# Four weight tiles loaded and turned by quarters, inverse tables turned in one visit, and a re-phased backward second step

## The chip, the cores and the metric

The kernel runs on one core of a Trainium2 chip. The metric is device time in microseconds (us) of one execution; lower is better. Engines are named as the profile names them: PE is TensorE (PEld its weight loads), DVE is VectorE, ACT is ScalarE, POOL is GpSimd, SP is SyncE, which here only issues DMAs.

## What is computed

A transformer block (a spectral mixer followed by a token-mixing MLP, both with pre-LayerNorm and residual) and all its gradients, from bf16 inputs:

```python
def _A_ref(x, w_r, w_i):                       # spectral mixer, S = 2048, D = 448
    X = rfft2(x.astype(float32), axes=(-2, -1))
    y = irfft2(X * (w_r + 1j * w_i), s=(S, D)).astype(bfloat16)
def _B_ref(x, w1, b1, w2, b2):                 # MLP over tokens, F = 1792
    u = einsum("bsd,sf->bdf", layernorm(x), w1) + b1
    y = einsum("bdf,fs->bds", gelu(u), w2) + b2
    return y.transpose(0, 2, 1)
h  = x + _A_ref(layernorm(x), w_r, w_i)
h2 = h + _B_ref(h, w1, b1, w2, b2)             # with a LayerNorm of h inside
out, vjp = jax.vjp(f, x, w_r, w_i, w1, b1, w2, b2)
return out, *vjp(grad_out)                     # 8 outputs
```

## The kernel before

The order on TensorE, VectorE, ScalarE and SP is written by hand: each engine runs its instructions in the program's order. Where the code calls `evac`, a running estimate of the load of the two engines chooses whether ScalarE or VectorE empties a PSUM bank, so a moved step can move an evacuation from one engine to the other. PSUM is eight banks, four called `ps_mm` (long accumulations) and four called `ps_ff` (everything short).

The stages, with the times at which TensorE is in them:

- Opening (0 to 49 us). The rows of x are normalised and put through the first step of the FFT, 16 row tiles t. `row_a(t)` is four 128x128 products of a folded pair of rows (`fold_prep` or `fold_quarters`, VectorE) with `Rs[t]` (`scale_R`, VectorE: the table `Rm` times the row's 1/std). `row_b(h)`, three tiles behind, is four products with the table `csF`. `csF` is made once: a sine on ScalarE, then two flips of it on VectorE, then a 2-element copy on ScalarE over the first column (`gen_fwd_d`, run at t = 1 from `cs_ops`). The tables `Ut` and `Vt` come in pieces from `gen_UV` (VectorE, with a sine each on ScalarE).
- Between these, `fill(n)` takes n steps of the generator `dg_gen`: dgu = w2 . grad_out, 14 tiles j of w2 by 16 products t, each 128x448, 224 steps in all. `FILL_A[t]` and `FILL_B[t]` say how many steps stand in row tile t behind `row_a(t + 1)` and at its end. A product needs tile j of w2 transposed. Tiles 0 to 4 are loaded as they lie (`load_w2T`, 512 KB each) and turned on TensorE (`turn_w2`: 16 transposes of 128x128 into PSUM, ScalarE copies them to SBUF); tiles 5 to 13 come through a DMA that transposes. The first 32 steps alternate between tiles 0 and 1 by quarters of four t, since grad_out also arrives by quarters. The ring `w2T_ring` has five places, so the load of tile 5 is issued when tile 0 has been used up, and so on.
- `gen_inv_s(a)` turns the tables Ut and Vt for the inverse: 32 products of 32x32 for each a, at t = 10, 11, 12 and 13. `gen_RT` turns a permuted copy of `Rm` at t = 2.
- Forward second step (`s2_stage`, 49 to 73 us): for each of four sets s, 48 products in 32x32 groups (`four`), four evacuations, `fill(n1)`, the second `four` of the set before, a multiplication by the spectral weights on VectorE, `fill(n2)`; a fifth round closes the last set.
- Inverse rows and LayerNorm of h, the MLP forward, its backward (76 to 225 us).
- Backward: rows of the FFT, `s2_stage` again (240 to 281 us) with `bwd_mult` on VectorE, then `inv_rows` with the gradient of x. `fill` takes its steps from two generators `gw_gen` here (gradients of w2 and w1, 196 and 224 steps). One period of `gw_gen` is 14 steps: six products of 128x128 weights, then one step with four products of 64-row groups (`parts`, two at a time side by side), one empty step, six more products. `N_FILL_B[2]` steps are filled ahead of the backward second step, `N_FILL_B[4]` behind it, `N_FILL_B[5]` in each inverse row; what is left is run by `drain` at the end. 28 steps are filled in the rows before `N_FILL_B[2]`.

SP's queue in the opening, in order: x tiles 0 and 1 (224 KB), w2 tile 0 (512 KB), x 2 and 3 (224 KB), grad_out quarter 0 (448 KB), w2 tile 1, x 4 to 7 (448 KB), grad_out quarters 1, 2 and 3, w2 tile 2, x 8 to 11, w2 tile 3, x 12 to 15, a 2 KB tail of grad_out, two bias loads, w2 tile 4, then the spectral weights W, mixed with the transposing loads and the reshapes of the rows (`resh`). Eight DMAs are in flight at most: each waits for the one eight places ahead to land.

20 dummy products of zeros run on TensorE at the start (L375).

## Time and profile before

Three runs took 340.55, 341.36 and 341.02 us, median 341.02. The profiled execution took 340.96 us; its span, from the first to the last instruction, is 339.2 us, so 1.76 us lie outside it. The profile comes from that execution.

| stretch (us) | stage | TensorE busy (us) | VectorE busy | ScalarE busy | DMA GB/s |
|---|---|---|---|---|---|
| 0 to 6.3 | dummies, first loads | 5.08 | 4.91 | 3.56 | 213 |
| 6.3 to 15.6 | rows, up to row_a(4) | 7.75 of 9.30 | 8.88 | 8.05 | 388 |
| 15.6 to 32.8 | rows, up to row_a(10) | 16.04 of 17.20 | 16.53 | 12.29 | 209 |
| 32.8 to 49.2 | last rows, tables | 16.36 of 16.40 | 10.43 | 11.46 | 230 |
| 49.2 to 76 | forward second step, rest of dg | 26.45 of 26.80 | 16.77 | 17.75 | 164 |
| 76 to 95 | inverse rows | 18.40 of 19.00 | 15.25 | 17.11 | 258 |
| 95 to 238.5 | MLP, backward rows | 143.5 of 143.5 | 98.62 | 64.39 | |
| 238.5 to 281 | backward second step | 42.32 of 42.50 | 36.88 | 31.38 | 241 |
| 281 to 326 | backward inverse rows | 45.00 of 45.00 | 36.16 | 34.68 | 263 |
| 326 to 339.2 | rest of gw, last stores | 9.41 of 13.20 | 8.18 | 5.52 | 246 |

Read it so: a product counts as busy until its result is out, so a busy TensorE can still lose time between two starts. The weight loads (PEld) show when a product could start.

### The profile page before, as it was taken

What the parts mean: (1) busy time and instruction counts of PE and PEld (TensorE: products, weight loads), DVE (VectorE), ACT (ScalarE), POOL (GpSimd) and SP (SyncE); (2) the same over time, 40 slices, a digit from 0 to 9 for tenths busy, and PEclk for the clock granted to TensorE, in tenths of its full rate; (3) what the DMA queues carried; (4) which work ended last, traced back from release to release, by engine and by line L of the source; (5) the groups of instructions that cost most, each with busy time, mean ns of one, the idle gap of its engine ahead of it and who ended that gap; (6) DMA issues with size and microseconds to landing.
All of it is one profiled execution on the core that took longest, in us unless ns stands there. A gap on an engine that the chain in (4) does not pass through costs nothing.

```text
span 339.2 us, 7995 instructions
## 1 busy us (share of the span) xinstructions
PE 330.3 (97%) x2893; PEld 174.0 (51%) x2893; DVE 252.6 (74%) x678; ACT 206.2 (61%) x447; POOL 83.9 (25%) x255
## 2 busy tenths in 40 slices
PE   8898999999999999999999999999999999999995
PEld 4565665456545555555555555555334344555552
DVE  8999649726947888594226988787598984599994
ACT  6886766858965544523132346665488875688882
POOL 7755602331310000000001111210002222156660
PEclk9999999999999999999999999999999999999999
DMA  7979999949999999787986989636998999969785
GB/s 250 399 195 183 228 245 196 167 110 261 252 366 305 337 277 241 179 259 197 187 192 154 188 176 165 171 83 203 262 254 280 184 227 281 349 164 295 233 309 198
DMA packets 136142, 78.03 MB, mean 230 GB/s; under 512 B 86568, under 2 KB 127512, under 8 KB 135976
## 3 DMA queue, kind: packets, MB, share of 16 engines
q1 hardware_dynamic: 133576, 73.59, 82.6%
q0 software_dynamic: 2528, 3.95, 5.5%
q8 instruction: 22, 0.36, 0.5%
q14 instruction: 16, 0.13, 0.2%
HBM read 28.33 MB, written 22.04 MB: 149 GB/s over the span
## 4 chain that ended last, share of the span: by engine, by line
PE 85%; DVE 6%; ACT 3%; DMA 2%; SPq 2%; issue 1%; POOL 0%; DVEq 0%; ACTq 0%
PE ps_mm L220 73%; PE ps_ff L220 8%; PE ps_ff L225 4%; DMA rA<-in_A_x_dram 2%; ACT rO L84 2%; DVE r L84 2%; DVE stats L84 1%; SPq L329 1%; SPq L310 1%; DVE rS L84 1%; DVE rA L84 1%; ACT rAT L84 0%; DVE rD L84 0%; DVE rX L84 0%; DVE rB L84 0%
## 5 line engine op out<-in xcount | busy, mean ns | idle before, releaser
L220 PEld LDWEIGHTS <-r 128*128 128x128 bf16 (+2 forms) x628 | 58.4, 104 | 47.6 <-issue 3.0
L220 PEld LDWEIGHTS <-rS 128*128 128x128 bf16 (+1 forms) x468 | 36.3, 97 | 33.4 <-issue 7.7
L84 ACT CAST rO<-ps_mm 128x512 bf16<-128x512 f32 (+1 forms) x69 | 36.9, 584 | 14.6 <-PE ps_mm L220 13.0
L220 PE MATMUL ps_mm<-rD,r 128*128 128x448 bf16 x224 | 44.5, 352 | 0.0
L220 PEld LDWEIGHTS <-rst 128*128 128x128 bf16 (+1 forms) x320 | 23.6, 97 | 31.3 <-issue 14.0
L731 POOL DMA_DIRECT2D r<-r x30 | 17.8, 601 | 66.5 <-ACT r L84 59.3
L220 PE MATMUL ps_mm<-rC,rE 128*128 128x448 bf16 x144 | 32.1, 353 | 0.5 <-DMA rC<-in_grad_out_dram 0.4
L220 PE MATMUL ps_mm<-rB,r 128*128 128x448 bf16 x160 | 31.2, 352 | 0.1
L220 PE MATMUL ps_mm<-rG,rst 128*128 128x512 bf16 (+1 forms) x128 | 28.7, 380 | 0.2 <-ACT rO L84 0.2
L220 PE MATMUL ps_mm<-r,rst 128*128 128x512 bf16 (+2 forms) x144 | 27.4, 345 | 0.0
L84 ACT ACTIVATE r<-ps_mm,rstd_h 128x448 bf16<-128x448 f32 x16 | 10.1, 633 | 26.8 <-PE ps_mm L220 26.8
L84 ACT CAST r<-ps_ff 128x452 bf16<-128x452 f32 x43 | 23.2, 589 | 4.5 <-PE ps_ff L225 2.1
L84 DVE SCALAR_TENSOR_TENSOR r<-ps_mm,b2col,r 128x448 bf16<-128x448 f32 x16 | 10.9, 682 | 19.9 <-PE ps_mm L220 19.8
L84 ACT ACTIVATE r<-rC 128x448 bf16<-128x448 bf16 x16 | 9.1, 571 | 26.7 <-DMA out_dram<-r 14.1
L1189 POOL TENSOR_SCALAR lcol<-lcol 128x1 f32<-128x1 f32 x16 | 8.5, 528 | 64.7 <-ACT r L84 64.7
L84 ACT ACTIVATE rG<-rG 128x896 bf16<-128x896 bf16 x14 | 13.3, 950 | 14.9 <-DVE rG L84 14.7
L220 PEld LDWEIGHTS <-rO 128*128 128x128 bf16 (+1 forms) x165 | 15.3, 98 | 12.2 <-ACT rO L84 0.2
L84 ACT CAST rS<-ps_ff 128x512 bf16<-128x512 f32 x31 | 18.1, 587 | 2.5 <-PE ps_ff L220 2.4
L220 PE MATMUL ps_ff<-csI,rAT 113*128 113x224 bf16 (+1 forms) x108 | 19.0, 298 | 0.4 <-ACT rAT L84 0.2
L84 DVE TENSOR_SCALAR rG<-rG 128x896 bf16<-128x896 bf16 x28 | 10.9, 388 | 10.0 <-ACT rG L84 10.0
L220 PE MATMUL ps_mm<-rC,rO 128*128 128x448 bf16 x80 | 18.1, 353 | 0.0
L84 ACT CAST rG<-ps_mm 128x512 bf16<-128x512 f32 (+1 forms) x28 | 13.8, 534 | 6.8 <-PE ps_mm L220 6.7
(202 smaller groups left out, 638.2 us busy)
## 6 DMA issues: line engine op xcount, KB each, us to landing
out_dram<-rO SPq DMA_DIRECT2D x34, 256.0 KB, 3.0
r<-in_B_w_dram SPq DMA_DIRECT2D x5, 1024.0 KB, 8.4
r<-r POOLq DMA_DIRECT2D x30, 113.0 KB, 5.4
out_dram<-rG SPq DMA_DIRECT2D x11, 256.0 KB, 3.7
r<-r SPq DMA_DIRECT2D x12, 226.0 KB, 2.5
r<-in_B_w_dram SPq DMA_DIRECT2D x3, 896.0 KB, 5.1
rS<-in_B_w_dram SPq DMA_DIRECT2D x3, 896.0 KB
rB<-in_B_w_dram SPq DMA_DIRECT2D x5, 512.0 KB, 9.8
```

Source lines behind the costliest of these rows:

```text
L84: fn(**kw)
L220: nc.tensor.matmul(out, lhsT=lhsT, rhs=rhs, start=start, stop=stop)
L225: nc.tensor.matmul(out, lhsT=lhsT, rhs=rhs, start=start, stop=stop)
L310: nc.sync.dma_start(out=w2n[j], in_=B_w2[j * P:(j + 1) * P, :].rearrange("f (t c) -> f t c", c=P))
L329: nc.sync.dma_start(out=go_tp[:, 4 * q:4 * q + 4, :], in_=go_tp_d[:, 4 * q:4 * q + 4, :])
L731: defer(RESH_LAG, lambda g=g, ab=ab, eng=eng: eng.dma_start(out=D3[rowbase(g):rowbase(g) + 29:4, :, :, :], in_=ab), ab)
L1189: gp_.tensor_scalar(out=m1, in0=ms, scalar1=-1.0 / D, scalar2=None, op0=ALU.mult)
```

## The change

Two constants, the loads and turns of the first w2 tiles, the places of some steps, and the fill counts change:

- w2 tiles 0 to 3 are loaded in eight quarters. `load_quarter(k)`, k = 2 q + p, brings columns of quarter q (four t) of the pair p (tiles 2p and 2p + 1): 256 KB in pieces of 1 KB. `turn_quarter(k)` turns these eight blocks and copies them to SBUF in one copy (the first in two). Tile 4 is loaded whole, into rD, and turned by halves (`turn_half`). All turns use `ps_ff`.
- `dg_gen` takes tiles 0 to 3 together by quarters: step n = 16 q + 4 j + i. Turns 1, 2 and 3, 4 and 5, 6 and 7 stand right behind steps 7, 15, 31 and 47, the halves of tile 4 behind 57 and 61. The loads of tiles 5 to 8 are issued behind steps 51, 55, 59 and 63.
- SP's queue becomes: x 0 and 1, quarter 0, grad_out 0, x 2 and 3, quarter 1, x 4 to 7, grad_out 1, quarters 2 and 3, x 8 to 11, grad_out 2, quarters 4 and 5, x 12 to 15, grad_out 3, quarters 6 and 7, tile 4, W. The tail of grad_out and the biases are loaded after the last rows.
- 10 dummy products at the start, two more ahead of `row_a(0)`; four dg steps now stand before `row_a(0)`, and FILL_A and FILL_B differ in the first nine tiles.
- `gen_inv_s` does all four a in one visit, behind the rows; `gen_RT` and its copies stand at t = 13.
- In the backward second step n1 is 14, n2 is 14, 28, 14, 28 and 20 by round (13 and 20 before), and 35 steps (26 before) are filled ahead of it.

```diff
--- before.py
+++ after.py
@@ -36,10 +36,10 @@
 ML_F = 4
 SIDE = 2
 CAP = 9
-N_NAT = 5
+N_QTR = 4
 U_Q = 2
 N_FILL_F = (6, 3, 20, 3, 24, 2)
-N_FILL_B = (16, 16, 26, 8, 24, 8)
+N_FILL_B = (16, 16, 35, 8, 24, 8)
 INV_SD = 1.0 / float(S * D)
 
 
@@ -298,7 +298,7 @@
 
     x_pt = A_x[0].rearrange("(p t) d -> p t d", t=NT)
     go_pt_d = grad_out[0].rearrange("(p t) d -> p t d", t=NT)
-    w2T_ring = Ring(ring(rE, 0, 3, NT, P).views + ring(rO, S, 2, NT, P).views)
+    w2T_ring = Ring(ring(rE, 0, 2, NT, P).views + ring(rO, S, 2, NT, P).views + [cut(rE, 2 * S, NT, P)])
 
     def load_w2T():
         j = w2T_ring.i
@@ -306,21 +306,44 @@
             return
         wT = w2T_ring.next()
         w2Ts[j] = wT
-        if j < N_NAT:
-            nc.sync.dma_start(out=w2n[j], in_=B_w2[j * P:(j + 1) * P, :].rearrange("f (t c) -> f t c", c=P))
+        if j < N_QTR:
+            return
+        if j == N_QTR:
+            nc.sync.dma_start(out=w2n4, in_=B_w2[j * P:(j + 1) * P, :].rearrange("f (t c) -> f t c", c=P))
             return
         nc.sync.dma_start_transpose(out=wT, in_=B_w2[j * P:(j + 1) * P, :].rearrange("f (t c) -> f t c", c=P))
 
-    def turn_w2(j, parts=((0, 8), (8, 8))):
-        for h, n in parts:
-            pt = (ps_mm if j < 2 else ps_ff)()[:].bitcast(BF16).rearrange("p (t c) -> p t c", c=P)
-            for t in range(n):
-                nc.tensor.transpose(pt[:, t, :], w2n[j][:, h + t, :], ident[:])
-            sc.copy(out=w2Ts[j][:, h:h + n, :], in_=pt[:, 0:n, :])
+    def turned():
+        return ps_ff()[:].bitcast(BF16).rearrange("p (t c) -> p t c", c=P)
+
+    def turn_half(h):
+        pt = turned()
+        for t in range(8):
+            nc.tensor.transpose(pt[:, t, :], w2n4[:, h + t, :], ident[:])
+        sc.copy(out=w2Ts[N_QTR][:, h:h + 8, :], in_=pt)
+
+    def turn_quarter(k):
+        q, p = divmod(k, 2)
+        pt = turned()
+        for t in range(8):
+            nc.tensor.transpose(pt[:, t, :], w2q[:, 2 * p + t // 4, 4 * q + t % 4, :], ident[:])
+        dst = w2pair[p][:, :, 4 * q:4 * q + 4, :]
+        if k:
+            sc.copy(out=dst, in_=pt.rearrange("p (j t) c -> p j t c", j=2))
+            return
+        for j in range(2):
+            sc.copy(out=dst[:, j], in_=pt[:, 4 * j:4 * j + 4, :])
+
+    def load_quarter(k):
+        q, p = divmod(k, 2)
+        src = B_w2[2 * p * P:(2 * p + 2) * P, :].rearrange("(j f) (t c) -> f j t c", f=P, c=P)
+        nc.sync.dma_start(out=w2q[:, 2 * p:2 * p + 2, 4 * q:4 * q + 4, :], in_=src[:, :, 4 * q:4 * q + 4, :])
 
     go_tp_d = grad_out[0].rearrange("(t p) d -> p t d", p=P)
     w2Ts = {}
-    w2n = [cut(rB, j % 4 * S, NT, P) for j in range(N_NAT)]
+    w2q = cut(rB, 0, 4, NT, P)
+    w2pair = [cut(rE, 0, 2, NT, P), cut(rO, S, 2, NT, P)]
+    w2n4 = cut(rD, 10 * 512, NT, P)
 
     def load_x(q):
         nc.sync.dma_start(out=xn[:, 4 * q:4 * q + 4, :], in_=x_pt[:, 4 * q:4 * q + 4, :])
@@ -329,21 +352,26 @@
         nc.sync.dma_start(out=go_tp[:, 4 * q:4 * q + 4, :], in_=go_tp_d[:, 4 * q:4 * q + 4, :])
 
     nc.sync.dma_start(out=xn[:, 0:2, :], in_=x_pt[:, 0:2, :])
-    load_w2T()
+    load_quarter(0)
+    load_go(0)
     nc.sync.dma_start(out=xn[:, 2:4, :], in_=x_pt[:, 2:4, :])
-    load_go(0)
-    load_w2T()
+    load_quarter(1)
     load_x(1)
     load_go(1)
+    load_quarter(2)
+    load_quarter(3)
+    load_x(2)
     load_go(2)
+    load_quarter(4)
+    load_quarter(5)
+    load_x(3)
     load_go(3)
-    load_w2T()
-    load_x(2)
-    load_w2T()
-    load_x(3)
+    load_quarter(6)
+    load_quarter(7)
+    for _ in range(N_QTR):
+        load_w2T()
     gtail = rst[0:16, 2 * P:3 * P]
     gp_.memset(gtail, 0.0)
-    nc.sync.dma_start(out=gtail[:, 0:64], in_=grad_out[0][S - 16:S, 3 * P:D])
 
 
     s1, s128, s2048 = 2.0 * _sin_scale(2), _sin_scale(128), _sin_scale(2048)
@@ -371,7 +399,7 @@
     sc.activation(out=warm, in_=warm, func=ACT.Sin)
     nc.vector.memset(rAT[:, 0:512], 0.0)
     idle = ps_mm()
-    for _ in range(20):
+    for _ in range(10):
         nc.tensor.matmul(idle[:, 0:D], lhsT=rAT[:, 0:P], rhs=rAT[:, 0:D], start=True, stop=True)
 
     pcol = col()
@@ -525,18 +553,19 @@
         mm(pt[:, 0:P], lhsT=Rp, rhs=ident[:], start=True, stop=True)
         evac(out=RTm[:], in_=pt[:, 0:P])
 
-    def gen_inv_s(a):
-        pt = ps_ff()
-        for w, src in enumerate((Ut, Vt)):
-            for x in range(4):
-                o = 32 * (4 * w + x)
-                for r in range(4):
-                    small(pt[blk(r + a & 3), o:o + 32], lhsT=src[blk(r), 8 * (x // 2) + 2 * a + x % 2, :], rhs=permI[blk(r), :],
-                          start=True, stop=True)
-        evac(out=UVT[:].rearrange("p w g m -> p (w g m)").rearrange("p (x a y) -> p a x y", x=4, a=4)[:, a],
-             in_=pt[:, 0:256].rearrange("p (x y) -> p x y", x=4))
-        if a == 3:
-            gen_neg(UTn[:], UTt)
+    def gen_inv_s():
+        uvt = UVT[:].rearrange("p w g m -> p (w g m)").rearrange("p (x a y) -> p a x y", x=4, a=4)
+        pts = [ps_ff() for _ in range(4)]
+        for a, pt in enumerate(pts):
+            for w, src in enumerate((Ut, Vt)):
+                for x in range(4):
+                    o = 32 * (4 * w + x)
+                    for r in range(4):
+                        small(pt[blk(r + a & 3), o:o + 32], lhsT=src[blk(r), 8 * (x // 2) + 2 * a + x % 2, :],
+                              rhs=permI[blk(r), :], start=True, stop=True)
+        for a, pt in enumerate(pts):
+            (ve.tensor_copy if a % 2 else sc.copy)(out=uvt[:, a], in_=pt[:, 0:256].rearrange("p (x y) -> p x y", x=4))
+        gen_neg(UTn[:], UTt)
 
     inv_cols = {}
 
@@ -735,7 +764,7 @@
                     on_mult(s, j, x[:, 2 * j:2 * j + 2], y[:, 2 * j:2 * j + 2])
             if after is not None and s in after:
                 after[s]()
-            fill(n2)
+            fill(n2[s])
         fill(gap)
 
     def gen_neg(dst, src):
@@ -812,6 +841,7 @@
 
     def load_biases():
         gp_.memset(smr, 0.0)
+        nc.sync.dma_start(out=gtail[:, 0:64], in_=grad_out[0][S - 16:S, 3 * P:D])
         nc.sync.dma_start(out=smr[0:NFB, 0, :], in_=B_b1.rearrange("(j p) -> j p", p=P))
         nc.sync.dma_start(out=smr[:, 1, :], in_=B_b2.rearrange("(j p) -> j p", p=P))
 
@@ -827,14 +857,16 @@
 
     def dg_gen():
         pgs = {}
-        turns = {(0, 3): 1, (1, 11): 2, (2, 4): 3, (3, 4): 4}
-        order = [(j, 4 * q + i) for q in range(4) for j in range(2) for i in range(4)]
-        for j, t in order + [(j, t) for j in range(2, NFB) for t in range(NT)]:
+        turns = {7: (1,), 15: (2, 3), 31: (4, 5), 47: (6, 7)}
+        order = [(j, 4 * q + i) for q in range(4) for j in range(N_QTR) for i in range(4)]
+        for n, (j, t) in enumerate(order + [(j, t) for j in range(N_QTR, NFB) for t in range(NT)]):
             if not t:
                 pgs[j] = ps_mm()
             mm(pgs[j][:, 0:D], lhsT=w2Ts[j][:, t, :], rhs=go_tp[:, t, :], start=(t == 0), stop=(t == NT - 1))
-            if (j, t) in turns:
-                turn_w2(turns[j, t], ((0, 4), (4, 4), (8, 8)) if j == 0 and t == 3 else ((0, 8), (8, 8)))
+            for k in turns.get(n, ()):
+                turn_quarter(k)
+            if n in (57, 61):
+                turn_half(2 * (n - 57))
             if t == NT - 1:
                 evac(out=dgu[:, j, :], in_=pgs.pop(j)[:, 0:D])
                 if w2T_ring.i >= cap[0]:
@@ -874,12 +906,14 @@
     fold_prep(xn, 0)
     ve.reciprocal(out=rstd_x[:, 0:2], in_=rstd_x[:, 0:2])
     Rs = {t: scale_R(t) for t in range(2)}
-    turn_w2(0, ((0, 4), (4, 4)))
+    turn_quarter(0)
+    for _ in range(2):
+        nc.tensor.matmul(idle[:, 0:D], lhsT=rAT[:, 0:P], rhs=rAT[:, 0:D], start=True, stop=True)
+    fill(4)
     row_a(0, Rs.pop(0))
     for t in range(2, 4):
         ln_stats(xn, t, mvx)
     sc.activation(out=rstd_x[:, 2:4], in_=mvx[:, 2:4, 1], func=ACT.Sqrt, bias=eps_x, scale=1.0)
-    turn_w2(0, ((8, 8),))
     fold_prep(xn, 1)
     cs_ops = []
     gen_fwd_d(cs_ops)
@@ -889,24 +923,17 @@
     uv = gen_UV()
     gen_inv_cols(0)
     gen_inv_cols(1)
-    fill(4)
     for t in (4, 5):
         ln_stats(xn, t, mvx)
     for fn in rstd_of(4, 6):
         fn()
     fill(0)
-    turn_biases, place_biases = load_biases()
     Meter.side, Meter.every, Meter.count = [], 1, 0
     GROUPS = {0: (6, 8), 1: (8, 10), 3: (10, 12), 5: (12, 14), 7: (14, 16)}
     STATS = {0: (6, 7), 1: (8, 9), **{t: (t + 8,) for t in range(2, 8)}}
-    INV_S = {10: 0, 11: 1, 12: 2, 13: 3}
     W_AT = {0: 2, 1: 1, 2: 2, 3: 1, 4: 2, **{t: 1 for t in range(5, 11)}, 11: 4}
-    for c in range(2):
-        for e in range(2):
-            sc.copy(out=Rp.rearrange("p (e a q b c) -> p c e a q b", e=2, c=2, q=8, a=2)[:, c, e],
-                    in_=Rm[:, 64 * c + 32 * e:64 * c + 32 * e + 32].rearrange("p (q a b) -> p a q b", q=8, a=2))
-    FILL_A = (4, 4, 8, 12, 6, 3, 3, 3, 3, 3, 3, 3, 3, 3, 3, 3)
-    FILL_B = (0, 0, 2, 2, 2, 2, 4, 4, 3, 2, 2, 2, 2, 2, 2, 2)
+    FILL_A = (4, 7, 9, 7, 1, 6, 2, 5, 4, 3, 3, 3, 3, 3, 3, 3)
+    FILL_B = (0, 0, 0, 0, 5, 3, 6, 4, 3, 2, 2, 2, 2, 2, 2, 2)
     for t in range(NT):
         if t == 0:
             load_w2T()
@@ -944,9 +971,11 @@
             newton_gp(mvx[:, a:b, 1], rstd_x[:, a:b], slice(a, b))
         for _ in range(W_AT.get(t, 0)):
             next(w_loads, None)
-        if t in INV_S:
-            gen_inv_s(INV_S[t])
-        if t == 2:
+        if t == 13:
+            for c in range(2):
+                for e in range(2):
+                    sc.copy(out=Rp.rearrange("p (e a q b c) -> p c e a q b", e=2, c=2, q=8, a=2)[:, c, e],
+                            in_=Rm[:, 64 * c + 32 * e:64 * c + 32 * e + 32].rearrange("p (q a b) -> p a q b", q=8, a=2))
             gen_RT()
         fill(FILL_B[t])
     for _ in uv:
@@ -960,12 +989,15 @@
     cap[0] = NFB
     while held_w2:
         held_w2.pop(0)()
-    fill(14)
+    turn_biases, place_biases = load_biases()
+    fill(8)
+    gen_inv_s()
+    fill(6)
 
     def fwd_mult(s, j, x, y):
         w_mult(x, set_of(W, s)[:, 2 * j:2 * j + 2], y, False)
 
-    s2_stage(lambda s: set_of(Xs, s), fwd_mult, 8, 8, 0, split=True)
+    s2_stage(lambda s: set_of(Xs, s), fwd_mult, 8, (8,) * 5, 0, split=True)
     sc.activation(out=warm, in_=eps_h, func=ACT.Sqrt)
     drain()
 
@@ -1350,7 +1382,7 @@
         rows(t)
     fill(N_FILL_B[2])
     Meter.slack = 7.0
-    s2_stage(lambda s: X_ring.next(), bwd_mult, 13, 20, N_FILL_B[4], {0: lambda: load_du(1), 1: lambda: (load_du(0), load_xall(0)), 2: lambda: load_xall(1), 3: lambda: load_du(2)},
+    s2_stage(lambda s: X_ring.next(), bwd_mult, 14, (14, 28, 14, 28, 20), N_FILL_B[4], {0: lambda: load_du(1), 1: lambda: (load_du(0), load_xall(0)), 2: lambda: load_xall(1), 3: lambda: load_du(2)},
              2.0 * INV_SD)
     Meter.slack = 2.0
     g_out = w_io(out_2, out_3, True)
```

## The prediction, made before the changed kernel ran

> **What bounds the kernel now.** I read the page's busy shares and chain first, then the order in time of each engine in the opening (0 to 50 us) and in the backward second step (235 to 285 us).
>
> ```profile
> PE 330.3 (97%) x2893; PEld 174.0 (51%) x2893; DVE 252.6 (74%) x678; ACT 206.2 (61%) x447; POOL 83.9 (25%) x255
> ...
> PE 85%; DVE 6%; ACT 3%; DMA 2%; SPq 2%; issue 1%; POOL 0%; DVEq 0%; ACTq 0%
> ```
>
> TensorE sets the end. The chain runs on it for 85%, and one piece of the chain (94.86 to 188.89 us) has no pause at all. So whatever TensorE loses or gains before 95 us moves the end by as much. Its pauses lie in the opening; in this view the last bracket is the idle time before a row and what ended it:
>
> ```profile
> 15.57 0.65 PE L220 MATMUL ps_ff<-rX,rS 128*128 128x128 bf16 x4 [0.78 <-DVE rS L84]
> ...
> 32.84 0.40 PE L220 MATMUL ps_ff<-rX,rS 128*128 128x128 bf16 x4
> ```
>
> These are row_a(4) and row_a(10); a third such wait, 1.01 us, stands at 30.81 (row_a(9)). After 32.84 nothing waits until the forward second step starts at 49.20. What feeds these rows is VectorE, and what ScalarE does meanwhile decides the case:
>
> ```profile
> 6.19 1.15 DVE L84 BATCH_NORM_STATS2 stats<-rA 128x6 f32<-128x448 bf16 x2 [0.20 <-DMA rA<-in_A_x_dram]
> ...
> 15.74 0.46 DVE L84 TENSOR_SCALAR csF<-csF,cols 128x224 bf16<-128x224 bf16 x2
> 16.44 1.15 DVE L84 BATCH_NORM_STATS2 stats<-rA 128x6 f32<-128x448 bf16 x2 [0.24 <-DMA rA<-in_A_x_dram]
> ```
>
> ```profile
> 16.29 0.20 ACT L84 COPY csF<-rAT 128x2 bf16<-128x2 bf16 x1 [1.08 <-DVE csF L84]
> 16.39 0.58 ACT L84 CAST rS<-ps_ff 128x512 bf16<-128x512 f32 x1
> 16.86 0.27 ACT L84 CAST RTm<-ps_ff 128x128 bf16<-128x128 f32 x1
> ...
> 17.50 1.95 ACT L84 COPY rE<-ps_ff 128x1024 bf16<-128x1024 bf16 x2
> ```
>
> From 6.19 on VectorE works without a pause down to the csF flip at 15.74, and ScalarE stands 1.08 us in its own queue, at 16.29, until that flip is done. Before the change that hurts nobody: tiles 0 and 1 of w2 were turned whole and copied by 11.7 us, so TensorE has 32 steps of dg that need no copy.
>
> **The opening, part by part.** I count dg steps from 0 and call the copy of quarter k "copy k".
>
> *Loads.* x tiles 2 and 3 move from third to fourth in SP's queue, with 928 KB ahead instead of 736. At the 277 to 362 GB/s of that stretch the 192 KB more are 0.5 to 0.7 us; I take 0.6. Bounds: 0 (the queue hides it) and 2.0, by which the first grad_out load, which ends TensorE's wait at 8.19, came later than the x load. VectorE has no slack behind this load, so all up to the flip moves with it: flip done at 16.2 + 0.6, R(2), scaled at 10.28 in the same order, ready at 10.5 + 0.6 = 11.1. The third x load comes earlier, which removes the 0.24 us before 16.44, behind the flip and so too late to help it. Fewer dummies (20 to 12) are worth nothing: row_a(0) waits for VectorE's scaled table at 6.0 anyway.
>
> *The new wait.* By program order TensorE now does 8 steps and turns 0 and 1, row_a(2) at 11.1 (0.22), seven steps (7 x 0.187 = 1.31), row_a(3) (0.22), step 15 (0.19), turns 2 and 3 (16 transposes, 0.90: the groups of 16 at 20.54 and 26.18 took 0.89). It stands at step 16 at 13.95. Step 16 needs copy 2. In ScalarE's queue that is: csF sine, the csF copy that waits for the flip, the cast of row_a(3), copy 2. So 16.39 + 0.6 = 16.99, cast 0.47 (start to start, 16.39 to 16.86), copy 0.97 (half of 1.95): 18.43. TensorE stands 4.5 us, and behind step 16 in its queue stands all the rest: rows 4 and on, and so VectorE's casts of them.
>
> *From there to row_a(10).* Steps 16 to 69 (54 x 0.187 = 10.1), 48 transposes (2.67), six row_a (1.32), six row_b at 0.40 (2.4): 16.5 us, to 34.95. Two waits come on top. Turns 4 and 5 follow step 31 and step 32 needs copy 4: TensorE is there at 18.45 + 16 steps 3.0 + 2 row_a 0.44 + 2 row_b 0.80 + turns 0.89 = 23.58, ScalarE ends copy 4 at 24.5 (cast of row_b(0) at 21.9 to 22.45, Ut's sine 0.62, cast of row_a(5) 0.47, copy 0.97): 0.95. Copy 6 the same way: 0.2. So row_a(10) at 36.1 instead of 32.84: **+3.3**. VectorE, without two rD casts (1.06) and with one ps_ff cast more (0.54), would have had its fold there at 32.8 - 0.24 - 1.06 + 0.54 + 0.6 = 32.6; it is not the bound any more.
>
> *Inverse tables in one go.* Each of the four visits (35.69, 37.47, 39.26, 41.03) starts 0.097 us late on the way into 32x32 groups and costs 0.09 on the way out, by the starts of its neighbours. Three visits fall away: **-0.56**. The last evacuations are covered by the six steps (1.1 us) before the second step; uncovered they cost two copies of 0.37. RT and its four copies move to t = 13, where nothing waits for ScalarE: 0.
>
> *Queue SP.* The tail of grad_out and two bias loads leave SP's opening and stand before the last three transposed loads; their users come 20 us later: 0. The transposed loads of tiles 5 to 8 start at step 51 instead of 28; step 51 comes at 30, the first use (step 80) at 39.6, issue takes 2.1 to 2.5 and landing 5.2: covered by some 2 us; uncovered, the shortfall is paid in full (bound +1). The x load that ends VectorE's wait at 16.44 closed 4.7 MB of the queue; quarters 4 and 5 now end at 4.2 MB and are turned at 22, quarters 6 and 7 at 5.6 MB (at 390 GB/s some 2.5 us behind it, 19) and are turned at 28: 0.
>
> **The backward second step.** The starts of weight loads show the price of a change of group shape:
>
> ```profile
> 249.86 0.11 PEld L220 LDWEIGHTS <-r 64*128 64x128 bf16 x4 [0.42 <-issue]
> ...
> 253.90 0.11 PEld L220 LDWEIGHTS <-r 64*128 64x128 bf16 x4 [0.42 <-issue]
> ...
> 257.14 0.11 PEld L220 LDWEIGHTS <-rst 64*128 64x128 bf16 x4 [0.42 <-issue]
> 257.67 0.14 PEld L225 LDWEIGHTS <-Vt 32*32 32x32 bf16 x16 [0.42 <-issue]
> ...
> 261.08 0.11 PEld L220 LDWEIGHTS <-rst 64*128 64x128 bf16 x4 [0.42 <-issue]
> 261.77 0.19 PEld L225 LDWEIGHTS <-UVT 32*32 32x32 bf16 x32 [0.58 <-DVE rS L84]
> ```
>
> From one 64-row group to the next are 3.24 us bare (253.90 to 257.14), 4.04 with a second step among whole products (249.86 to 253.90), 3.94 with one right behind the 64-row group (257.14 to 261.08). Two of eight stand so already; six more save 6 x 0.10 = **-0.6**. The stage before also lost 0.16 (261.77 came 0.69 behind 261.08, not 0.53) and 0.34 (a 64-row product at 270.01 behind ScalarE's backlog). After, three forward groups have ScalarE clear four second-step tiles right behind two output tiles, as at 257.67 where 0.16 followed: 3 x 0.16 = 0.48 against 0.50, no change. y of set 0 is ready 10.5 us behind its forward group (240.04 to 250.54), the next use now comes at 3 x 3.24 + 0.71 + 0.71 = 11.1: just covered. Bounds for the stage: -1.1 and +0.5. The 18 fills done earlier leave 31 instead of 49 for the end; the last rows' VectorE chain (13 operations, one a fill) is still covered.
>
> **Sum.** +3.3 - 0.56 - 0.6 = **+2.1**, on the profiled execution's 340.96 (span 339.2 and 1.76 around it), which is 0.06 under the median 341.02: 343.1. Its own range, 341.6 to 344.8, takes in the x load's bounds (-0.6, +1.4) and the stage's.
>
> **Rivals.**
> *The clock falls in the pause* (344.3). In the opening dummies take 0.37 us each up to 4.2 us and 0.19 after, and the clock share of the last 13.2 us is 0.98, half speed for 0.5 us, which begins 3.3 us behind the last product (335.4). The longest pause before is 1.4 us; the new one is 4.5. A fall would cost what the opening's slow stretch does (1.2 to 4.2, 3.0 us at half speed: 1.5), less 0.3 that the wait for copy 4 takes back: +1.2. [...]
> *ScalarE's hold does not bite* (339.5). If copy 2 came by 13.9, because the flip or its copy doesn't stand before it, TensorE would follow VectorE: row_a(10) at 32.6 (-0.3), then -0.56 - 0.6: -1.5. It decides where copy 2 is done before 16.3, 2.1 us earlier than worked out. For it: VectorE is the one that ended the pauses of before. Against it: the 1.08 us at 16.29 and ScalarE's order.
> *The groups do not fall behind the 64-row groups* (343.7). The steps done before the stage are 28 + 35 = 63 = 4 x 14 + 7, the seventh of a period of 14 is the 64-row one, and all later fills are multiples of 14; against it only a miscount.
>
> **How the numbers follow.** Chances: forecast 0.47, clock 0.28, no hold 0.17, groups 0.08. The forecast's low end reaches no change. About 0.2% (0.7 us) is what a measurement can tell. Faster 0.15, same 0.10, slower 0.75. The range, 340.3 to 346.0, leaves out most of the no-hold case below and a fall of the clock that lasts two stretches above.
>
> **What would show it.** TensorE idle some 4.5 us before a dg product on rE near 18.4 us, ended by ScalarE's rE copy; 0.9 near 24.5; ScalarE's csF copy held again by VectorE until about 16.9; the forward second step at 51.9 instead of 49.20; one visit to the inverse tables; eight 32x32 groups 0.53 behind a 64-row load. Wrong: no pause over 2 us between 13 and 19 us, or a start of the second step by 49.5.

## The result: slower by 10 to 15 us, and the profile after

The changed kernel took 350.36, 355.25, 356.12 and 354.3 us, median 354.77; the kernel before, beside it, 340.85 (four runs). The ratio is 1.036, 95% interval 1.028 to 1.043. Medians here and below are over all runs; each ratio leaves out the runs that took over 1.5% longer than the fastest of the same kernel, here the one of 356.12. The forecast was 343.1: slower is right, the size is not. The profiled execution is the one of 350.36 us; its span is 348.6, so 1.8 us lie around it and 9.4 us of span are to be explained, and 4 to 6 more in the other three runs.

First the page of the changed kernel: busy time by engine, the queue that carries instructions, and the engines' shares of the chain.

```profile
PE 331.9 (95%) x2885; PEld 176.0 (50%) x2885; DVE 253.1 (73%) x679; ACT 206.5 (59%) x445; POOL 83.2 (24%) x255
...
q8 instruction: 22, 0.36, 0.5%
...
PE 79%; DVE 6%; DMA 6%; ACT 5%; issue 2%; SPq 1%; DVEq 0%; POOL 0%; ACTq 0%
```

TensorE's share of the chain falls from 85 to 79%: DMA has 6 instead of 2, ScalarE 5 instead of 3, and "issue" (no releaser in the profile) 2 instead of 1. Where it stands shows in the starts on TensorE (us, both profiled executions):

| | before | after | later by | forecast |
|---|---|---|---|---|
| row_a(2) | 11.24 | 12.05 | 0.81 | 11.1 |
| dg step 16 | 13.45 | 19.36 | 5.91 | 18.43 |
| row_a(10) | 32.84 | 39.20 | 6.36 | 36.1 |
| forward second step | 49.20 | 57.71 | 8.51 | 51.9 |
| last dh product | 224.68 | 232.66 | 7.98 | |
| end of the last product | 335.41 | 343.31 | 7.90 | |
| end of the span | 339.15 | 348.58 | 9.43 | 341.3 |

TensorE's order in the opening of the changed kernel; the last bracket is its idle time and what ended it.

```profile
12.05 0.40 PE L220 MATMUL ps_ff<-rX,rS 128*128 128x128 bf16 x4 [2.69 <-DVE rX L84]
...
19.36 2.83 PE L220 MATMUL ps_mm<-rC,rE 128*128 128x448 bf16 x8 [2.63 <-ACT rE L84]
...
27.30 1.12 PE L220 MATMUL ps_mm<-rC,rE 128*128 128x448 bf16 x5 [0.93 <-ACT rE L84]
...
32.90 1.31 PE L220 MATMUL ps_mm<-rC,rE 128*128 128x448 bf16 x6 [0.26 <-ACT rE L84]
...
47.44 0.23 PE L220 MATMUL ps_ff<-ident,rO 128*128 128x128 bf16 x1 [1.19 <-ACT rO L84]
...
56.67 1.11 PE L220 MATMUL ps_mm<-rC,rO 128*128 128x448 bf16 x5 [0.90 <-issue]
```

The second, third and fourth lines are the forecast's waits for copies 2, 4 and 6. For copies 4 and 6 the idle time shown is 0.93 and 0.26; from start to start they cost 1.09 (25.81 to 27.30, less 0.40 for a row_b) and 0.42 (32.08 to 32.90, less the same), where the forecast had 0.95 and 0.2. The fifth is the RT product, which waits for ScalarE's four copies of Rm; the last is the product behind the visit to the inverse tables, which waits for nothing that has a name. Both were priced at nothing. Why copy 2 is late is on ScalarE, and so are the four copies for RT (last line):

```profile
17.72 0.20 ACT L84 COPY csF<-rAT 128x2 bf16<-128x2 bf16 x1 [2.66 <-DVE csF L84]
17.82 0.58 ACT L84 CAST rS<-ps_ff 128x512 bf16<-128x512 f32 x1
18.29 1.01 ACT L84 COPY rE<-ps_ff 128x1024 bf16<-128x1024 bf16 x1
...
46.81 0.57 ACT L84 COPY rO<-Rm 128x32 bf16<-128x32 bf16 x4
```

This is the hold that was forecast, copy behind cast behind the two-element copy that waits for VectorE's flip, but at 17.72, 0.8 later than the 16.9 of the forecast. And the clock fell. Busy time in four stretches of 3.41 us; the third number from the right is the granted clock, and ahead of it stand TensorE, its weight loads, VectorE, ScalarE and GpSimd.

```profile
9.52:12.93 3.41, 0.88 (x8) 0.61 (x9) 3.31 (x14) 1.61 (x3) 2.73 (x13) 1.00 1.07 391
12.93:16.34 3.41, 3.41 (x22) 2.33 (x21) 3.10 (x16) 2.10 (x4) 1.23 (x6) 0.50 1.08 379
16.34:19.76 3.42, 0.79 (x9) 0.43 (x8) 3.38 (x14) 2.04 (x4) 2.68 (x11) 1.00 1.09 385
19.76:23.17 3.41, 3.41 (x14) 1.64 (x13) 3.19 (x11) 0.98 (x2) 2.73 (x13) 0.50 1.15 144
```

A stretch in which TensorE was busy for 0.8 or 0.9 us of its 3.41 is followed by one at half speed, twice.

The backward second step, weight loads of the changed kernel:

```profile
249.76 0.11 PEld L220 LDWEIGHTS <-rS 64*128 64x128 bf16 x4 [0.42 <-issue]
250.30 0.14 PEld L225 LDWEIGHTS <-Vt 32*32 32x32 bf16 x16 [0.42 <-issue]
...
260.88 0.11 PEld L220 LDWEIGHTS <-r 64*128 64x128 bf16 x4 [0.42 <-issue]
261.53 0.19 PEld L225 LDWEIGHTS <-UVT 32*32 32x32 bf16 x32 [0.54 <-issue]
```

The 32x32 groups do stand behind the 64-row groups, 0.54 and 0.65 us behind their load. What came with it is a wait of TensorE for a transpose of du, 0.73 us longer between starts than without it:

```profile
290.05 1.90 PE L220 MATMUL ps_mm<-r,rst 128*128 128x512 bf16 x10 [0.57 <-DMA r<-rD]
```

### The profile page after: what moved, and what is told of

It reads as the page before. It is cut to its first block, busy times and chain, and to the rows that moved or that the text cites. A ratio compares the mean times of both kernels' runs of the same rounds, so it can differ in the third digit from the quotient of the medians.

```text
span 348.6 us, 7987 instructions
## 1 busy us (share of the span) xinstructions
PE 331.9 (95%) x2885; PEld 176.0 (50%) x2885; DVE 253.1 (73%) x679; ACT 206.5 (59%) x445; POOL 83.2 (24%) x255
## 4 chain that ended last, share of the span: by engine, by line
PE 79%; DVE 6%; DMA 6%; ACT 5%; issue 2%; SPq 1%; DVEq 0%; POOL 0%; ACTq 0%
PE ps_mm L220 67%; PE ps_ff L220 7%; PE ps_ff L225 4%; DVE r L84 3%; DMA r<-rD 2%; ACT rO L84 2%; DMA rA<-in_A_x_dram 2%; DMA r<-r 1%; DVE stats L84 1%; ACT rE L84 1%; ACT rAT L84 1%; DMA out_dram<-rG 1%; DVE rA L84 1%; ACT r L84 0%; DVE rS L84 0%
## 5 line engine op out<-in xcount | busy, mean ns | idle before, releaser
L84 ACT CAST rO<-ps_mm 128x512 bf16<-128x512 f32 (+1 forms) x63 | 34.1, 581 | 15.0 <-PE ps_mm L220 13.7
L220 PE MATMUL ps_mm<-rC,rE 128*128 128x448 bf16 x128 | 30.3, 364 | 4.1 <-ACT rE L84 3.8
L220 PE MATMUL ps_mm<-rG,rst 128*128 128x512 bf16 (+1 forms) x128 | 27.8, 380 | 0.0
L220 PEld LDWEIGHTS <-rO 128*128 128x128 bf16 (+1 forms) x181 | 17.4, 99 | 17.0 <-issue 2.0
L84 ACT ACTIVATE r<-rC 128x448 bf16<-128x448 bf16 x16 | 9.1, 570 | 26.9 <-DMA out_dram<-r 14.1
L220 PE MATMUL ps_mm<-rC,rO 128*128 128x448 bf16 x96 | 22.6, 368 | 0.9 <-issue 0.9
L84 ACT CAST rS<-ps_ff 128x512 bf16<-128x512 f32 x29 | 16.8, 580 | 7.9 <-PE ps_ff L220 7.8
L84 ACT CAST rG<-ps_mm 128x512 bf16<-128x512 f32 (+1 forms) x33 | 16.6, 550 | 7.8 <-PE ps_mm L220 7.7
L84 DVE CAST rO<-ps_mm 128x512 bf16<-128x512 f32 x17 | 11.6, 690 | 10.4 <-PE ps_mm L220 10.3
```

The costliest lines, as they stand in the source:

```text
L84: fn(**kw)
L220: nc.tensor.matmul(out, lhsT=lhsT, rhs=rhs, start=start, stop=stop)
```

## The experiments

Diffs show their core. "Step 16" and the like are starts on TensorE; medians are of the runs with their lowest and highest.

### The pause in the opening: hold, load and clock

Dummies in the pauses:

```diff
+            if n == 15:                 # dg_gen, behind turns 2 and 3
+                spin(22)
+        if t == 1:                      # row loop, ahead of row_a(2)
+            spin(12)
```

> The changed kernel with dummy products of zeros (128x448) put into two pauses of TensorE in the opening: 12 ahead of row_a(2) and 22 behind turns 2 and 3, ahead of dg step 16. They write a bank that nobody reads; nothing else changes. Clock theory (the overrun is in good part half-speed windows that the idle stretches bring on, and which window falls on what differs from run to run): no half-speed window between 6 and 30 us, step 16 still near 19.4 because ScalarE's copy ends then, row_a(10) 1.5 to 2 us earlier than 39.20, time 348 to 349 us and the runs within 1 us of each other. Rival (the clock costs nothing beyond what ScalarE's queue sets anyway): row_a(10) within 0.4 us of 39.20, times spread from 350 to 356 as without the dummies.

Step 16 at 19.17, row_a(10) at 37.33 instead of 39.20, no half speed up to 290 us. TensorE's order there:

```profile
14.67 4.32 PE L883 MATMUL ps_ff<-rAT 128*128 128x448 bf16 x22
19.17 1.69 PE L220 MATMUL ps_mm<-rC,rE 128*128 128x448 bf16 x8 [0.18 <-ACT rE L84]
```

The eight products of 19.17 take 1.69 us instead of the 2.83 they took in the changed kernel: the clock cost 1.87 us at row_a(10). Median 349.31 (347.33 to 355.09, ratio 1.018, 1.011 to 1.025). The spread stays, and the run of 355.09 shows another source: 5.07 us of idle time in the backward second step, ended by the transpose of du.

```profile
292.22 3.50 PE L220 MATMUL ps_mm<-r,rst 128*128 128x512 bf16 x10 [5.07 <-DMA r<-rD]
```

The hold taken away:

```diff
-        Later(sc, late).copy(out=csF[:, 0, :, 0:1], in_=rAT[:, 0:2].rearrange("p (b o) -> p b o", o=1))
+        v_.tensor_copy(out=csF[:, 0, :, 0:1], in_=rAT[:, 0:2].rearrange("p (b o) -> p b o", o=1))
```

> The changed kernel with one instruction moved: the two-element copy over the first column of csF goes from ScalarE's queue to VectorE's, right behind the flips. ScalarE-hold theory (step b of the prediction): copy 2 starts by 15.6 instead of 18.29, step 16 at about 16.6 instead of 19.36, row_a(10) 2 to 3 us earlier than 39.20, and with a pause under the 3.4 us of a clock window fewer half-speed windows: 346 to 349 us. Rival (copy 2 is not what TensorE lacked, or VectorE sets the rows as before): step 16 within 0.5 us of 19.4 or row_a(10) within 0.7 us of 39.2, time above 350.

Copy 2 starts at 15.43, step 16 at 16.50, row_a(10) at 36.80, 2.4 earlier, with no half speed before 75 us. So the hold was what TensorE waited for. The median is 349.74 (347.96 to 352.28), not 346 to 349: the profiled run lost 3 us again at 74.48, of which below.

The x load alone moved back (one execution, 351.91 us):

```diff
     load_quarter(0)
-    load_go(0)
     nc.sync.dma_start(out=xn[:, 2:4, :], in_=x_pt[:, 2:4, :])
+    load_go(0)
```

> The changed kernel with the load of x tiles 2 and 3 back in third place of SP's queue, ahead of the first quarter of grad_out. Load theory (step a of the prediction, priced 0.6, measured 1.43): VectorE's statistics of these tiles start at 6.2 to 6.4 instead of 7.60, the flip of csF ends 1.2 to 1.4 us earlier, copy 2 starts near 17.0 instead of 18.29, step 16 near 18.1 instead of 19.36; the first dg step comes 0.5 to 1.5 later and that costs nothing. Rival: another thing ends the flip's wait, step 16 within 0.4 of 19.36.

Copy 2 at 17.13 and step 16 at 18.20, as the theory said, 1.16 earlier; but row_a(10) at 38.89 gains only 0.3, since now two half-speed stretches in a row fall on the work behind it (mean granted clock of the execution 0.987). Load and clock taken out together:

```diff
-    load_go(0)
     nc.sync.dma_start(out=xn[:, 2:4, :], in_=x_pt[:, 2:4, :])
+    load_go(0)
...
-    for _ in range(2):                  # ahead of fill(4) and row_a(0)
+    for _ in range(8):
...
+            if n == 15:
+                spin(20)
```

> The changed kernel with x tiles 2 and 3 back in third place of SP's queue, six more dummy products ahead of the first dg step and 20 ahead of step 16, so that the load and the clock are taken out and the order of ScalarE's queue is left as it is. If the forecast's step from the hold to row_a(10) was right and only the load (0.8) and the clock (1.9) were missing: no half-speed window between 7 and 30 us, step 16 at 18.0 to 18.4, row_a(10) at 36.0 to 36.6 (forecast 36.1). Rival (some other loss sits in these rows): row_a(10) at 37.3 or later.

The single execution took 347.85 us; the granted clock is whole up to 342 us, step 16 at 18.16, and

```profile
24.42 1.12 PE L220 MATMUL ps_mm<-rC,rE 128*128 128x448 bf16 x5 [0.94 <-ACT rE L84]
...
36.31 0.39 PE L220 MATMUL ps_ff<-rX,rS 128*128 128x128 bf16 x4
```

36.31 against the forecast's 36.1. That they lie so close is in part luck. The forecast has 0.6 in it for the load, which is back in its place here (ScalarE's csF copy is at 16.50, 0.2 behind the kernel before), so step 16 comes 0.3 earlier than forecast; and from step 16 to row_a(10) are 18.15 us where the forecast adds up 17.67, most of the difference in the waits for copies 4 and 6 (1.09 and 0.42). So the 6.36 us at row_a(10) are 3.47 of the hold and the copy waits (36.31 - 32.84), 1.02 of the later load (37.33 - 36.31) and 1.87 of the clock.

### RT and the inverse tables

RT and its four copies back at their old places in the program:

```diff
+    for c in range(2):                  # the copies, ahead of the row loop
...
-        if t == 13:
-            for c in range(2):
...
+        if t == 2:
             gen_RT()
```

> The changed kernel with gen_RT back at t = 2 and its four copies of Rm back ahead of the row loop. RT theory: the wait of 1.19 us ahead of the RT product at 47.44 is gone and comes back nowhere, the first forward second step starts 1.1 to 1.4 us earlier than 57.71 (less up to 0.5 if the four copies, 0.5 us on ScalarE early, delay copy 1 or copy 2). Rival (another engine, VectorE's table pieces or a DMA, holds the rows by then): under 0.4 us gained.

The four runs took 351.03 (350.51 to 359.25, ratio 1.026, 1.020 to 1.033); the profiled one is that of 359.25. The wait ahead of the RT product is gone, but the second step starts at 58.15: the wait behind the visit to the inverse tables grew from 1.08 to 1.93, and the clock took more in this execution (mean granted share 0.978, 0.989 in the changed kernel). From row_a(10) to the second step it is 17.96 us instead of 18.51. The cost of RT is thus shown by its own bracket, not by the end. The visit split into four again (`INV_S` as before):

```diff
+        if t in INV_S:                  # {10: 0, 11: 1, 12: 2, 13: 3}
+            gen_inv_s(INV_S[t])
...
-    fill(8)
-    gen_inv_s()
-    fill(6)
+    fill(14)
```

> The changed kernel with the inverse tables turned again in four visits, at t = 10, 11, 12 and 13 (32 products each), instead of one visit of 128 ahead of the second step. [...] Prediction's term (one visit is worth 0.56): the second step starts 0.56 later than in the changed kernel, 58.3, and the wait at 56.67 stays.

The wait behind the visit is gone and the second step starts at 57.30, the part from row_a(10) down from 18.51 to 17.53; the visit at one go cost more than it saved (some 0.4 of the 0.98 is a shorter wait of the RT product). All four runs are at 355.6 to 356.0; in the profiled one, 355.59, a wait of 4.1 us stands in the second step. The one visit alone, in the kernel before:

```diff
-        if t in INV_S:
-            gen_inv_s(INV_S[t])
...
-    fill(14)
+    fill(8)
+    gen_inv_s()
+    fill(6)
```

> The kernel before with one part of the change alone: the inverse tables turned in one visit ahead of the last six fills before the second step. Prediction's term: 0.56 us gained, second step at 48.6, time 340.4. [...]

There it waits 0.86 us inside the visit, and row_a(14), where a visit stood, waits 1.15 us for VectorE: 342.77 beside 342.51, ratio 1.0005 (0.997 to 1.004). Its second step starts at 50.93, not at the forecast's 48.6: the gain of 0.56 doesn't appear.

### The waits without a releaser

They cost most in the second step. In the run with RT moved back:

```profile
79.70 0.41 PE L225 MATMUL ps_ff<-rS,UTn 32*32 32x226 bf16 x15 [4.57 <-issue]
```

> The changed kernel with w2 tiles 9 to 13 loaded as they lie instead of through the transposing DMA, so that the gradient that uses them is left wrong; the same bytes in longer pieces, everything else in its place. DMA-backlog theory (TensorE's next block of program queues behind the 256-byte pieces of these loads, hence waits of 3.0 and 4.7 us inside a 32x32 group in two of the profiled executions and none in others): no wait of over 0.3 us in the forward second step, the time's spread over the runs falls to 1 to 2 us and the median by 2 to 4 us, to 350 to 352. Rival (the wait has nothing to do with these loads): the spread stays 5 us and waits without a releaser stay in the second step.

Tiles 9 to 13 then lie unturned, so this kernel leaves out what turns them, and the gradient made from them is not the one asked for; the bytes loaded are the same.

```diff
-        nc.sync.dma_start_transpose(out=wT, in_=src)
+        (nc.sync.dma_start_transpose if j < 9 else nc.sync.dma_start)(out=wT, in_=src)
```

350.57 (350.15 to 350.73): the spread is gone, and no such wait is in its second step. Ten to twenty us behind the start of the second step, in two stretches of 5 us; the DMA share stands second from the right. The changed kernel:

```profile
67.71:72.71 5.00, 5.00 (x114) 2.46 (x113) 3.79 (x9) 4.14 (x11) 2.43 (x5) 1.00 1.58 233
72.71:77.71 5.00, 5.00 (x71) 2.43 (x69) 3.75 (x8) 4.23 (x10) 2.28 (x5) 1.00 0.76 162
```

with the plain loads:

```profile
67.65:72.65 5.00, 5.00 (x114) 2.46 (x113) 3.79 (x9) 4.14 (x11) 2.44 (x5) 1.00 0.37 100
72.65:77.65 5.00, 5.00 (x71) 2.48 (x69) 3.75 (x8) 4.23 (x10) 2.35 (x5) 1.00 0.35 96
```

and the kernel before:

```profile
59.20:64.20 5.00, 5.00 (x113) 2.40 (x112) 3.97 (x9) 4.14 (x10) 2.38 (x5) 1.00 1.16 199
64.20:69.20 5.00, 4.65 (x68) 2.20 (x67) 3.76 (x8) 3.75 (x9) 1.84 (x4) 1.00 0.56 99
```

The same work on TensorE, with a DMA share of 1.58, 0.37 and 1.16 beside it. The kernel before is not free of the wait: its 4.65 in the last line is one of 0.57 us at 66.43. Nor does the share alone decide: the changed kernel's profiled execution had 1.58 and no such wait. The three small loads on SP are not the reason:

```diff
+    turn_biases, place_biases = load_biases()
     Meter.side, Meter.every, Meter.count = [], 1, 0
...
-    turn_biases, place_biases = load_biases()
     fill(8)
```

> The changed kernel with the tail of grad_out and the two bias loads back in the opening, ahead of the row loop, so that they no longer stand on SP between the transposing loads of w2 tiles 9 to 13. SP-order theory (the three loads, 1.5 us of SP's queue, push the last two transposing loads into the part of the second step where TensorE needs new program every 5 us): the last transposing loads issue 1 to 1.5 us earlier and the wait without a releaser near 74 to 80 shrinks by that or goes; median 351 to 353. Rival (the three loads do not matter, the loads are late because the tiles before them are used up late): the wait stays 2 to 5 us, median 354 to 356.

354.63 (350.78 to 355.1), with 2.1 us of such a wait at 76.49 and then 3.41 us at half speed. But the loads of tiles 5 to 8 wait on SP until tiles 0 to 3 are used up: from 30 to 35 us the DMA share is 0.07, before the change 0.82. Places of their own for them:

```diff
-    w2T_ring = Ring(ring(rE, 0, 2, NT, P).views + ring(rO, S, 2, NT, P).views + [cut(rE, 2 * S, NT, P)])
+    w2T_ring = Ring(w2T_at + ring(rG, 0, 4, NT, P).views + w2T_at)   # w2T_at: the five old places
...
-            load_w2T()                  # at t = 0
+            for _ in range(3):
+                load_w2T()
```

> The changed kernel with places of their own (the region rG, unused until the MLP) for the transposed tiles 5 to 8, so that their loads no longer wait on SP until tiles 0 to 3 are used up; the loads of 5 and 6 are issued behind tile 4, tiles 9 to 13 take the five old places. DMA-hole theory (the loads held back until step 51 leave the DMA engines idle at 28 to 34 us and push 2 MB of 256-byte pieces against the second step, where TensorE's program is then late): DMA share over 0.6 from 25 to 35 us, under 0.8 ten to twenty us behind the start of the second step, no wait of 2 us or more without a releaser in it, median 350 to 351.5 and a spread under 1.5 us, as with the plain loads. Rival (the transposing loads of tiles 9 to 13 alone make it late, whatever came before): the wait stays, 353 to 356.

The hole is filled (0.89 and 0.83 from 25 to 35 us), the median falls to 350.50 (349.73 to 352.67), but the profiled run, the slowest, has a wait of 2.9 us at 76.77, which the theory excluded, and the DMA share from 65 to 75 us is still 0.80 and 1.16. The hole is at most part of it.

What all these waits share is their place in the program. Counted in products from the start, they stand behind the 477th (the product behind the visit in six profiles of changed kernels, a table product in the kernel before with the one visit) or the 860th (a UTn product in six, one record short in one of them, a UVT product in the kernel before). 860 - 477 = 383, three times 128 but for one. The instruction queue of the page above has 22 packets, 0.36 MB, that is 16 KB each; if they carry TensorE's 5,770 products and loads, that is some 131 products with their loads to a packet, which I call a block. The trace agrees with this estimate: in the changed kernel the ninth to the fourteenth packet start when 1,122, 1,230, 1,352, 1,484, 1,606 and 1,744 products have started. In the run of the 4.57 us the block for that place starts to come in at 77.05, when TensorE had stood since 74.87; in the profiled execution of the changed kernel at 72.08, ahead of need. Counted in products, that packet starts at the 764th with the plain loads and at the 816th in the changed kernel (no wait in either), at the 826th and 838th in two runs that wait 2.0 and 1.9 us, and only when TensorE has come to the 860th in the four that wait 2.8 to 4.6 us. The count is not all of it: a later kernel waits 1.26 us with a start at the 805th, but there the packet takes 2.55 us instead of about 1. Behind the visit the packet is not late in this sense: it starts at 54.15 and takes 1.03 us, the visit's first product starts at 54.22, and 1.2 us later all its 128 products have started; what TensorE then lacks until 56.67 no trace shows. I call all of these waits for program, which is inferred from their places and from the packets, since no trace names what ends them. If they are, moving the program by some products must move them:

```diff
-    for _ in range(10):
+    for _ in range(4):
         nc.tensor.matmul(idle[:, 0:D], lhsT=rAT[:, 0:P], rhs=rAT[:, 0:D], start=True, stop=True)
+    for i in range(70):                 # 38 and 102 in the other two
+        nc.tensor.matmul(idle[blk(i & 3), 0:32], lhsT=rAT[blk(i & 3), 0:32], rhs=rAT[blk(i & 3), 0:32], start=True, stop=True)
```

> The changed kernel with six of its ten dummy products at the start replaced by 38 products of 32x32, so that every later product stands 32 places further in the program; all else is as changed. Block theory (TensorE runs dry at the end of a 16 KB block, 128 products and their weight loads, when the next block is late): waits without a releaser stand again behind product 477 and 860 by the new count, that is 32 products earlier in the work: the first inside the visit to the inverse tables, about 55.1 instead of 56.67, the second ahead of or in the first products of the second-step group at 73.9 instead of 74.5. Rival (the wait belongs to these instructions): it stays at the product behind the visit and at the UTn products.

> As the run before with 70 products of 32x32 (64 places). Block theory: the first wait falls inside the visit about 54.8, the second, if there is one, at the Ut products of the last forward group, 71.7 (old product 796) or at a later block, 78.3 (old product 924); none at the product behind the visit or at the UTn products of 74.5. Rival: both stay where they were.

> As the two before with 102 products of 32x32 (96 places). Block theory: the first wait falls inside the visit about 54.4, the second among the dg products at 70.2 (old product 764) or in the second-step group at 77.9 (old product 892); the time of the three shifted kernels differs from the changed kernel's 350 to 356 by what the next block finds: where the boundary stands ahead of slow products (dg, 0.19 us each) the wait is short. Rival: both stay where they were, 350 to 356 in all three.

With 32 places there is no such wait; with 64 and 96 one, behind product 605 by the new count, which is 477 + 128, first a dg product and then a Ut product. With 64 places:

```profile
61.02 1.12 PE L220 MATMUL ps_mm<-rC,rO 128*128 128x448 bf16 x5 [0.66 <-issue]
```

and with 96:

```profile
60.23 0.28 PE L225 MATMUL ps_ff<-r,Ut 32*32 32x226 bf16 x5 [2.06 <-issue]
```

At the old places nothing waits any more. So all three of the places that I expected were missed; what held is that the old places are free of waits and that both new waits stand 128 products behind 477. Each is one profiled execution of a kernel whose waits come and go, so the rival is refuted by the waits at 605, on products that never waited before, more than by the free old places. Medians 350.86 (350.18 to 354.51), 350.85 (350.11 to 354.44) and 352.96 (349.99 to 354.92): the spread of each is as wide as the gain, so the places are shown, and the gain of a shift is not. The profiled execution with 32 places took 354.51 without a wait for program: it lost its time at the transpose of du.

```profile
292.83 2.95 PE L220 MATMUL ps_mm<-r,rst 128*128 128x512 bf16 x10 [2.17 <-DMA r<-rD]
```

A stretch at half speed follows it, at 293.43. So a wait for du, as in the run of 355.09 above, makes a run of 354 to 355 us as well as a wait for program does.

### The backward counts

Alone in the kernel before:

```diff
-N_FILL_B = (16, 16, 26, 8, 24, 8)
+N_FILL_B = (16, 16, 35, 8, 24, 8)
...
-    s2_stage(lambda s: X_ring.next(), bwd_mult, 13, 20, N_FILL_B[4],
+    s2_stage(lambda s: X_ring.next(), bwd_mult, 14, (14, 28, 14, 28, 20), N_FILL_B[4],
```

> The kernel before with nothing but the backward counts of the change: 35 fills ahead of the backward second step instead of 26, n1 14 instead of 13, n2 14, 28, 14, 28, 20 by round instead of 20. Prediction's term: the stage gains 0.6 us (bounds -1.1 to +0.5) and the tail nothing: 340.2. By the trace after: the stage gains 0.2 to 0.3 and the tail behind the last product grows by 1.5 since 18 fills fewer are left to cover it: 341.9 to 342.3. If the tail stays at 3.7 us, its growth belongs to something else of the change.

342.89 beside 341.02, ratio 1.003 (1.000 to 1.007). The products wait 1.39 us for the transpose of du at 282.60, and the end:

```profile
336.27 0.39 DVE L84 TENSOR_TENSOR r<-r,rA 128x448 bf16<-128x448 bf16 x1
336.58 1.02 DVE L84 CAST rG<-ps_mm 128x512 bf16<-128x512 f32 x2
```

In the kernel before VectorE's last row operation is done by 332 and its last cast starts at 335.45. With 31 steps left instead of 49 the rows end at 336.7, behind the last product (336.19), and the last output waits for VectorE: the tail is 5.53 us instead of 3.74, in the changed kernel 5.27. The same phase with fewer steps done early:

```diff
-N_FILL_B = (16, 16, 35, 8, 24, 8)
+N_FILL_B = (16, 16, 21, 8, 24, 8)
```

> The kernel before with the backward counts of the change but 21 fills ahead of the backward second step instead of 35: the same phase behind the 64-row groups (28 + 21 = 49 = 3 x 14 + 7), 14 steps less done by then. Late-transposes theory (in the run with 35 the gain of the phase is there, but the products of the second gradient come before the transpose of du that is issued behind the last forward group, and the end has too few steps left to cover VectorE's last rows): no wait of a gradient product for du, tail behind the last product back at 3.7 us (45 steps left, 49 before), time 340.2 to 340.6, 0.4 to 0.6 under the kernel before. Rival (the phase itself is worth nothing): no faster than the kernel before by 0.2.

No wait for du, tail 3.74, and from the last dh product to the end of the last one 110.0 us against 110.73 before: the phase gains 0.7. The time doesn't show it: 341.2 beside 340.98, ratio 0.9995 (0.997 to 1.002); the opening differed by more in the profiled run. Inconclusive as a time.

### All mended

The edits shown above put together, with 21 fills and these dummies:

```diff
+            if n in (15, 31,):
+                spin({15: 6, 31: 8}[n])
```

> The quartered loads and turns and the fills of the opening as changed, and all else taken back or mended: csF column copy on VectorE, x tiles 2 and 3 third in SP's queue, dummy products where TensorE still pauses, gen_RT at t = 2, four visits to the inverse tables, biases in the opening, 21 fills ahead of the backward second step. If the losses are the ones named (hold, load, clock, RT, program fetch, du and tail), what is left is the copy waits of the opening: row_a(10) at 34.5 to 36, second step at 51 to 52.5, 342.5 to 345 us. If more is lost than named: over 346. If the quartered opening is worth something by itself: under 340.

Row_a(10) at 35.57 as expected, but the second step at 54.51 and 346.16 (344.6 to 347.4), ratio 1.008 (1.004 to 1.012): TensorE stood 2.52 us ahead of the first group, until the last 1.8 KB piece of the rows' reshape landed at 54.49. With the places for tiles 5 to 8:

> The mended kernel of the run before (csF copy on VectorE, x load third, dummies, RT and inverse tables and biases back, 21 fills) with the same places for tiles 5 to 8. In the mended kernel the first forward group waited 2.5 us until the last reshape of the rows landed, 5.3 us behind its issue against 2.9 in the kernel before. DMA-hole theory: the reshape lands 3 to 4 us behind its issue, that wait shrinks under 1 us, second step at 52 to 52.8, 342.5 to 344.5 us: the rest are the copy waits of the opening. Rival: the wait stays, 344.6 to 347.4 as before.

Second step at 51.76, no wait there, 342.29 (341.54 to 347.0), ratio 1.003 (0.999 to 1.007). Nearly all of the loss is thus named; the quartered opening itself is no gain, and at most about 2 us of loss. The same two lines of places, put into the kernel before, with the 21 fills:

> The kernel before with the places for tiles 5 to 8 and the backward counts with 21 fills. If the loads of the kernel before are early enough as they are, no change by the places: within 0.3 us of the run with 21 fills alone, that is no difference from the kernel before that can be told. If late program costs the kernel before something too (0.57 us at 66.43 in its profile) and the phase is worth its 0.6: 0.5 to 1.2 us faster than the kernel before.

341.04 beside 340.79, 0.9987 (0.995 to 1.002): no difference that can be told. The places move the loads of tiles 5 to 8 there by only 1 to 2 us (20.5 to 37.4 instead of 22.9 to 38.4), and its profile has a wait behind product 860, of 1.26 us at 67.42. No kernel tried beats the one before.

## Why the prediction was wrong in size

The side was right, and its main mechanism too: step 16 waits for copy 2 behind the csF copy. Taken alone it costs 3.47 us at row_a(10), where the forecast had 3.3 with 0.6 for the load in it, so 2.7. "ScalarE's hold does not bite" is refuted by the run without it; the groups do fall behind the 64-row groups. The 9.43 us of the profiled span, term by term:

| term | forecast | measured | where it shows |
|---|---|---|---|
| hold and copies | +2.7 | +3.5 | load and clock taken out |
| later x load | +0.6 | +1.0 | dummies with and without it |
| clock | rival, +1.2 | +1.9 | dummies in the pauses |
| RT | 0 | +1.4 | start-to-start at 47.44 |
| inverse tables | -0.56 | -0.3, then +1.1 waiting behind product 477 | 56.67 and the rest of that part |
| second step to the last dh product | 0 | -0.5 | differences 8.51 and 7.98; the kernel before waits 0.57 at 66.43 |
| phase | -0.6 | about -0.8 | 7.98 to 7.90, less the next row |
| transpose of du | 0 | +0.7 | 290.05 |
| tail | 0 | +1.5 | 9.43 - 7.90 |

Five steps failed.

- *Loads*, 0.6, was sized too small: VectorE waited 1.43 us longer for x tiles 2 and 3 (1.63 at 7.60, 0.20 at 6.19 before), of which 1.0 shows at row_a(10). The copy waits were sized 0.36 too small, as said above.
- "*The clock falls in the pause*" was kept apart from the sum with 0.28. It is no other case: in each of the ten profiles that have the pause the clock fell, for two stretches of 3.41 us, so it belonged in the sum.
- Covers were priced at nothing by the last user's time. RT "where nothing waits for ScalarE" is wrong (ScalarE starts the four copies at 46.81, behind its queue). "The last rows' VectorE chain (13 operations, one a fill) is still covered" counted the steps left, not the time at which VectorE's last row ends. The transposes of du were not priced at all, though 35 steps instead of 26 bring their user closer.
- "*Queue SP* ... covered by some 2 us" asked whether the first user of tile 5 would wait. It didn't. The cost was that these loads were issued at 33.9 to 45.2 us instead of 22.9 to 38.4, and all transposing loads behind them later against the stage (the last one leaves SP 14.1 us behind the start of the second step, 11.3 before), where TensorE runs 32x32 groups and the packets of the instruction queue start at 58.56, 63.84, 72.08 and 76.79, on average 6.1 us apart. In the traced runs with the biases or the inverse tables moved back (354.5 and 355.6) this is 4 to 6 us, wait and half speed behind it. Of the changed kernel itself only the run of 350.36 is traced, without that wait. That its other three runs lost their 4 to 6 us so is inferred, and a rival stands: the runs of 355.09 and 354.51 lost theirs waiting for du (5.07 and 2.17 us of idle time, and half speed behind it).
- *Inverse tables in one go*, -0.56, looked at the changes of shape and not at 128 products and their loads in 1.2 us, with the wait of 1.08 us behind them.

Open: why a block is late in one run and not in the next of the same kernel, how much of that the hole from 30 to 35 us explains, and which of the two waits the changed kernel's three untraced runs had.

## What to carry to other kernels

A pause that a change opens on TensorE can cost more than itself: here the two of 2.69 and 2.63 us were each followed by 3.41 us at half speed, 1.87 us more at row_a(10), so put the clock in the sum. When a load is said to be covered, ask also what the DMA engines do instead (a share of 0.07 from 30 to 35 us here, of 1.58 from 67.71 to 72.71) and what else must come through them then, the instruction queue's packets (22 of 16 KB here) included. Steps filled early are steps missing at the end: check the time of the other engines' last work, not the count of steps that hides it.
